# A two-workload kernel on one NeuronCore: the place of the Exp pass, of the attention copies and of one product in its rounds

## The chip, the cores and the metric

The kernel runs on one core of one Trainium2 chip. The metric is the device time in microseconds. Of the kernel before there are three timed runs (948.39, 950.51 and 950.9 us) and one profiled execution.

## The reference

Two independent computations share one launch. The first is chunked softmax attention, without a link between chunks:

```python
scores = scale * np.matmul(q_c, k_c.transpose(0, 1, 2, 4, 3))   # 8 x 8 x 9 chunks of 64 x 64
scores = scores - np.max(scores, axis=-1, keepdims=True)
attn = np.exp(scores)
attn = attn / (np.sum(attn, axis=-1, keepdims=True) + 1e-09)
out = np.matmul(attn, v_c)
```

Its result, turned to 4608 tokens of 512, is the input of the second:

```python
gate = 1.0 / (1.0 + np.exp(-(x @ w_gate)))      # 512 -> 1536
val = x @ w_val
return (gate * val @ w_out).astype(np.float32)  # 1536 -> 512
```

All values are float32. Every product of the second part is made of three matmuls over halves of the numbers (high x high, high x low, low x high).

## The kernel before

The tokens form nine blocks of 512. Blocks 0 to 2 are computed directly: for each of 12 slices `f` of the hidden width, `up` (L264) makes the gate and the value product, 12 matmuls each, `hidden` (L270) makes sigmoid times value and its two halves, and `down` (L290) adds 12 matmuls of the output product into four PSUM banks. `evacuate` (L297) copies them out (`ob`, L308).

Blocks 3 to 8 form three groups `n` of two blocks. A group replaces eight products of 2 x 2 parts by seven (numbered 1 to 7), on sums of operands and of weights that are made beforehand. The twelve rounds `i` of a group are its six values of `p`, each for `which` = 0 (gate) and 1 (value). A product is six matmuls of 128x512. A round runs on PE as `first` (products 1 and 6 into the banks `cx` and `cy`), then `last` of the round before (3 and 4), then `middle` (7, 2 and 5; product 5 has a PSUM bank of its own, `cz`, of which there is one). On ACT a round has the copy `s1` (L463) of product 1 and, where `which` is 0, four sigmoids (L495, L514). DVE adds: `u2` (L465), `u3` (L492), `c22` (L498), `c12` and `c21` (L508, L511). In odd rounds a gate product follows each (L475), three of the four on POOL. After the rounds `outward` (L526) does the output product, 252 matmuls at L579, from 21 operands that `prepare` casts (ACT, L551 and L559), takes the low half of (DVE, L552 and L560) and combines in place (DVE, L568).

Attention and the making of the next group's operands run beside all this. `flow` (L637) is a generator of small pieces in a fixed order. For two units of 512 x 512 it yields the score products `sc`, maximum and subtraction (L659, L660), the Exp pass (L663), sums and normalisation (L681 to L686), two transposes (L690), sixteen copies into `pbd` (L701 on POOL, L703 on ACT), the value products `av` (L234) and their copy (L245). Then come `differ` and `operands` (L407, L414) for the next group. `tick` (L714) spends credits, a number of each place in a round (`SHARES`), on these pieces; `insert` (L729) puts the products of attention between those of a round. Words such as "piece" or "wait" hold a piece back until a tick has passed, pairs such as ("up", n) until a group or a round is reached.

The order of PE, DVE and ACT is the order in which the program is written. The order of POOL and of SP, which issues all DMAs one after the other, is set by a scheduler. `keep_sums` (L334) is POOL's: it makes the sums of weights, some as `a_both` during blocks 1 and 2, the late ones as `a_late` in group 0, and SP stores them to DRAM. SP loads a round's weights (`wr`, L387 and L390) one round ahead. ACT loads another function table (ACT_TABLE_LOAD) between a sigmoid and an Exp.

Of the kernel before, what the change touches and what calls it, by code (L numbers as in the profile page):

```python
# [43 lines left out]

SHARES = {1: 2.7, 2: 3.0, "first": 0.7, "last": 2.0, "middle": 2.5, "down": 0.8}

# [4 lines left out]
def chunk_attn_moe(ctx: ExitStack, tc: tile.TileContext, q, k, v, w, out, outt):  # L51
# [362 lines left out]
    def operands(n):  # L414


        low = None
        for i, (name, (u, b), less) in enumerate(MADE):
            if i in (2, 5):
                yield from lower(*low)  # L420
                low = None
                yield ("open" if i == 2 else "up", n)
            at = raw[n, u][:, :, b]
            if less:
                (u0, b0), (u1, b1), op = less
                yield 1.2
                nc.vector.tensor_tensor(out=at, in0=raw[n, u0][:, :, b0], in1=raw[n, u1][:, :, b1], op=op)
            t = wp.tile([P, 2, 2, TB], F32R, tag=f"u{i}", name="xc")
            nc.scalar.copy(t[:, 0], at)
            if low:  # L430
                yield from lower(*low)
            low = n, name, t, at
        yield from lower(*low)
# [43 lines left out]
    def middle(n, p, which):  # L477
# [5 lines left out]
        if (p, which) == (0, 0):  # L483
            z = banks.pop((n, "z"), None) or sole(n, p, which)
            product(n, p, which, 2, x, False, True)
            product(n, p, which, 7, y, False, True)
        else:
            product(n, p, which, 7, y, False, True)
            product(n, p, which, 2, x, False, True)
            z = sole(n, p, which)  # L490
        u3 = mp.tile([P, TB], F32, tag="ob", name="u3")
        nc.vector.tensor_tensor(out=u3, in0=y, in1=s1, op=ALU.add)  # L492
        c22 = inner(n, f + 1, 1) if which == 0 else u3
        if which == 0:
            nc.scalar.activation(inner(n, f, 0), x, AF.Sigmoid)  # L495
        else:
            gated(n, f, 0, x, nc.vector)
        nc.vector.tensor_tensor(out=c22, in0=z, in1=u3, op=ALU.add)  # L498
        if which:
            gated(n, f + 1, 1, u3)  # L500
        banks[n, p, which] = y, z, s1, u2

# [23 lines left out]
    def outward(n, before_last):  # L526
# [14 lines left out]
        def prepare(i):  # L541
# [20 lines left out]
            if i == 3:  # L562
                reduce_hidden(n, 2, nc.vector)
            if i in (3, 4, 5, 9, 10, 11, 15, 16, 17):
                b11, t1x, b21, t2x = hid[n, i % 3]
                o, x, y, op = (
                    (b11, t2x, b11, ALU.subtract), (b21, b21, t2x, ALU.subtract), (t1x, t2x, t1x, ALU.add))[i // 6]
                nc.vector.tensor_tensor(out=o, in0=x, in1=y, op=op)  # L568
# [47 lines left out]
        for i in range(21):  # L616
# [6 lines left out]
            if i == 17 and n + 1 < 3:  # L623
                places[:] = [t2, t4, t0, t1, t3]
                load_group(n + 1, 0, 0)
            if i < 18:
                tick(SHARES["down"])
# [9 lines left out]
    def flow():  # L637
# [3 lines left out]
        for j in range(8, 4 * NB + 2, 2):  # L641
            more = j < 4 * NB
            joined = now["joined"]
            if more:
# [11 lines left out]
                for i in range(2):  # L656
# [4 lines left out]
                        out=pr[:, i], in0=scv[i], in1=mx.unsqueeze(2).broadcast_to([P, 8, D]), op=ALU.subtract)  # L661
                pr = pr.rearrange("p u g k -> p (u g) k")
                nc.scalar.activation(pr, pr, AF.Exp, scale=0.125)  # L663
            if kept and not (more and joined):
# [29 lines left out]
            for n in range(16):  # L694
                if n % 8 == 0:
                    yield "piece"
# [8 lines left out]
    ahead = flow()  # L705
    now = dict(credit=0.0, ticks=0, since=0, unit=8, early=-1, open=-1, up=-1, joined=False)
    now["item"] = next(ahead)
# [5 lines left out]

    def tick(share):  # L714
        now["ticks"] += 1
        now["credit"] += share
        while now["item"] is not None:
            if isinstance(now["item"], float):
                if now["credit"] < now["item"] / 2:
                    return  # L720
                now["credit"] -= now["item"]
            elif not (now["item"] == "piece" and now["ticks"] > now["since"]
                      or now["item"] == "wait" and now["ticks"] > now["since"] + (not now["joined"])
                      or now["item"][0] in ("early", "open", "up") and now["item"][1] <= now[now["item"][0]]):
                break
# [61 lines left out]
    def rest():  # L787
        for m in range(1, FIRST_PAIR):
            upto = 4 * (m + 2) if m == 1 else 4 * (m + 3)
            for f in range(2 if m == 1 else 0, NF):  # L790
                if m == 2 and f == 7:
                    now["early"] = now["open"] = now["up"] = 0
                step(m, f, "")
                tick(SHARES[m])
                insert(upto, 2)
                finish()
                tick(SHARES[m])
                insert(upto, 2)
                x = 12 * m + f - 13
                keep(min(32, (17 * x) // 10 if x < 11 else 17 + (17 * (x - 10)) // 10))  # L800
                if m == 2:
# [3 lines left out]
        for n in range(3):  # L805
            now["joined"], now["up"] = True, n
            upto = 4 * (FIRST_PAIR + 2 * n + 4)
            order = [(p, which) for p in range(6) for which in range(2)]
            due(n, 5)
            for i, (p, which) in enumerate(order):  # L810
# [11 lines left out]
                if i:  # L822
                    tick(SHARES["first"])
                    insert(upto, 1)
                    last(n, *order[i - 1])
                    if i == 10:
                        ending = outward(n, lambda: last(n, *order[-1]))
                        next(ending)
                    tick(SHARES["last"])
                    insert(upto, 1)  # L830
# [3 lines left out]
                if i == 11:  # L834
                    now["open"] = n + 1
                if n == 0 and i in (1, 2):
                    keep(32 + 2 * i, True)
                if 0 < i < 11:
                    tick(SHARES["middle"])
                    insert(upto, 1)  # L840
            next(ending, None)
# [37 lines left out]
```

## Time and profile before

| | us |
|---|---|
| timed runs, median (lowest to highest) | 950.51 (948.39 to 950.9) |
| profiled execution, its own time | 952.24 |
| its span in the trace | 950.5 |
| PE busy in the span | 913.1 (96%) |
| DVE, ACT, POOL busy | 577.5, 428.6, 320.4 |
| mean granted clock of PE, of full speed | 0.986 |

The profile shows one execution. In a timeline row stand the start, the duration of the merged instructions, the engine, the line, the operation with output and input, the number of instructions, and in brackets the idle time of the engine just before with what released it. PE's loads of weights (PEld) overlap its matmuls.

### The profile page before, as it was taken

What the parts mean: (1) busy time and instruction counts of PE and PEld (TensorE: products, weight loads), DVE (VectorE), ACT (ScalarE), POOL (GpSimd) and SP (SyncE); (2) the same over time, 40 slices, a digit from 0 to 9 for tenths busy, and PEclk for the clock granted to TensorE, in tenths of its full rate; (3) what the DMA queues carried; (4) which work ended last, traced back from release to release, by engine and by line L of the source; (5) the groups of instructions that cost most, each with busy time, mean ns of one, the idle gap of its engine ahead of it and who ended that gap; (6) DMA issues with size and microseconds to landing.
All of it is one profiled execution on the core that took longest, in us unless ns stands there. A gap on an engine that the chain in (4) does not pass through costs nothing.

```text
span 950.5 us, 13156 instructions
## 1 busy us (share of the span) xinstructions
PE 913.1 (96%) x4852; PEld 746.3 (79%) x4852; DVE 577.5 (61%) x818; ACT 428.6 (45%) x740; POOL 320.4 (34%) x421
## 2 busy tenths in 40 slices
PE   6999999999999997999999899999998999999998
PEld 4788788888888886887777788877777888888786
DVE  6889873454343458355557976455668854344784
ACT  6799652545545552344434432344435422113341
POOL 1000007999269979563330000242410001423000
PEclk7999999999999999999999899999999999999999
DMA  8698894445443465786654468764434685554563
GB/s 288 200 305 281 303 319 135 131 141 159 117 150 111 156 199 204 235 288 204 196 203 142 161 228 283 236 211 169 173 127 167 217 302 180 201 182 169 169 230 111
DMA packets 90544, 189.62 MB, mean 200 GB/s; under 512 B 7920, under 2 KB 49392, under 8 KB 86640
## 3 DMA queue, kind: packets, MB, share of 16 engines
q1 hardware_dynamic: 90480, 188.78, 59.9%
q8 instruction: 39, 0.64, 0.3%
q14 instruction: 25, 0.20, 0.1%
HBM read 146.28 MB, written 42.47 MB: 199 GB/s over the span
## 4 chain that ended last, share of the span: by engine, by line
PE 75%; DVE 9%; ACT 5%; DMA 5%; issue 2%; SPq 1%; POOL 1%; ACTq 0%; DVEq 0%
PE d L579 18%; PE g L264 14%; PE cy L447 13%; PE cz L447 9%; PE cx L447 9%; PE acc L290 6%; PE sc L173 3%; PE av L234 3%; DMA w_raw<-w_in 2%; DVE pr L660 1%; DMA given<-w 1%; DVE mx L659 1%; DVE w L139 1%; DMA wr<-sums 1%; ACT pr L663 1%
## 5 line engine op out<-in xcount | busy, mean ns | idle before, releaser
L264 PE MATMUL g<-xt,w 128*128 128x512 f32 (+1 forms) x960 | 209.2, 372 | 3.2 <-ACT hf L273 1.1
L264 PEld LDWEIGHTS g<-xt,w 128*128 128x128 f32 x960 | 168.3, 190 | 38.7 <-ACT hf L273 3.2
L579 PE MATMUL d<-hd,wd 128*128 128x512 f32 x756 | 177.4, 396 | 4.9 <-ACT hd L559 3.6
L579 PEld LDWEIGHTS d<-hd,wd 128*128 128x128 f32 x756 | 144.9, 192 | 37.0 <-ACT hd L559 4.4
L447 PE MATMUL cy<-xc,wr 128*128 128x512 f32 x648 | 161.9, 392 | 9.3 <-DVE s1u L465 5.2
L447 PEld LDWEIGHTS cy<-xc,wr 128*128 128x128 f32 x648 | 121.3, 188 | 37.0 <-DVE s1u L465 6.9
L475 POOL TENSOR_TENSOR hid<-u,hid 128x512 f32<-128x512 f32 x15 | 19.3, 1289 | 299.8 <-DVE u L498 299.6
L447 PE MATMUL cz<-xc,wr 128*128 128x512 f32 x432 | 111.3, 393 | 8.1 <-DVE u L498 6.0
L447 PE MATMUL cx<-xc,wr 128*128 128x512 f32 x432 | 111.3, 393 | 0.0
L290 PE MATMUL acc<-w,hx 128*128 128x512 f32 x432 | 106.2, 393 | 0.0
L352 POOL TENSOR_TENSOR a_val<-w 128x256 f32<-128x256 f32 x64 | 48.4, 777 | 165.0 <-DVE pbd L223 141.5
L447 PEld LDWEIGHTS cz<-xc,wr 128*128 128x128 f32 x432 | 80.1, 188 | 29.3 <-DVE u L498 8.5
L447 PEld LDWEIGHTS cx<-xc,wr 128*128 128x128 f32 x432 | 81.7, 190 | 17.8 <-issue 0.7
L290 PEld LDWEIGHTS acc<-w,hx 128*128 128x128 f32 x432 | 79.9, 188 | 18.0 <-issue 1.4
L275 DVE TENSOR_TENSOR hf<-g,hf 128x512 f32<-128x512 f32 (+1 forms) x40 | 25.4, 635 | 99.5 <-PE g L264 71.5
L559 ACT CAST hd<-hid 128x1024 fp32r<-128x1024 f32 x48 | 49.9, 1051 | 50.7 <-PE d L579 47.8
L560 DVE TENSOR_TENSOR hd<-hid,hd 128x1024 fp32r<-128x1024 f32 x48 | 58.4, 1224 | 18.6 <-ACT hd L559 18.6
L703 ACT COPY pbd<-pr 32x256 f32<-32x256 f32 x160 | 64.5, 403 | 11.4 <-DVE pr L690 9.5
L465 DVE TENSOR_TENSOR s1u<-cy,s1u 128x512 f32<-128x512 f32 x36 | 24.8, 688 | 72.1 <-PE cy L447 63.2
L463 ACT COPY s1u<-cx 128x512 f32<-128x512 f32 x36 | 21.0, 583 | 81.4 <-PE cx L447 81.4
L514 ACT ACTIVATE hid<-hid 128x512 f32<-128x512 f32 x54 | 33.3, 631 | 40.2 <-DVE hid L508 33.5
L475 POOL TENSOR_TENSOR hid<-s1u,hid 128x512 f32<-128x512 f32 x30 | 41.2, 1376 | 22.3 <-DVE s1u L508 21.6
(120 smaller groups left out, 1153.3 us busy)
## 6 DMA issues: line engine op xcount, KB each, us to landing
wr<-sums SPq DMA_DIRECT2D x72, 512.0 KB, 4.6
wd<-stream SPq DMA_DIRECT2D x30, 1024.0 KB, 4.8
w_raw<-w_in SPq DMA_DIRECT2D x36, 512.0 KB, 5.4
wr<-given SPq DMA_DIRECT2D x36, 512.0 KB, 3.7
sums<-a_both SPq DMA_DIRECT2D x24, 512.0 KB, 3.5
qt<-q_in SPq DMA_DIRECT2D x36, 256.0 KB, 4.1
kbd<-k_in SPq DMA_DIRECT2D x72, 128.0 KB, 3.9
vt<-v_in SPq DMA_DIRECT2D x36, 256.0 KB, 4.0
```

The lines of the kernel that those rows point to most:

```text
L173: nc.tensor.matmul(sc[c * D:(c + 1) * D, (2 * a + t) * P:(2 * a + t + 1) * P], lhsT=s["qt"][:, a, n0:n0 + D], rhs=s["kb"][:, a, :, n0:n0 + D],
L234: nc.tensor.matmul(av[a * D:(a + 1) * D, c * P:(c + 1) * P], lhsT=s["vt"][:, a, c, :], rhs=pb[:, 4 * a + c, :, :], start=True, stop=True,)
L264: nc.tensor.matmul(ps[:, tok], lhsT=wt[f, which][:, wpart, c:c + P], rhs=x[:, part, i, tok], start=n == 0, stop=n == 11)
L290: nc.tensor.matmul(acc[m, t], lhsT=hx[:, ts], rhs=wt[f, 2][:, wpart], start=f == 0 and i == 0, stop=f == NF - 1 and i == 2,)
L352: nc.gpsimd.tensor_tensor(out=dst, in0=parts[:, 0], in1=parts[:, 1], op=ALU.add)
L447: nc.tensor.matmul(bank, lhsT=lhs(wpart, c), rhs=x[:, part, c], start=start and k == 0, stop=stop and k == 5, skip_group_check=True)
L475: eng.tensor_tensor(out=h, in0=value, in1=h, op=ALU.mult)
L514: nc.scalar.activation(h, h, AF.Sigmoid)
L559: nc.scalar.copy(t[:, 0], at)
L560: nc.vector.tensor_tensor(out=t[:, 1], in0=at, in1=t[:, 0].bitcast(F32), op=ALU.subtract)
L579: nc.tensor.matmul(bank, lhsT=w[:, o:o + P], rhs=x[:, part], start=p == 0 and opening and i == 0, stop=p == 5 and i == 2, skip_group_check ...
L703: nc.scalar.copy(pb[dst, :, c, h, i, :], ps[src, h::2, k, :])
```

## The change

Five things are different.

A round of a group has three ticks, "first", "last" and "middle". In `flow`, a mark "apart" now stands ahead of the Exp pass, and `tick` doesn't pass it at "middle", only at the other two. The copies into `pbd` are one piece where groups run instead of two, and are kept from "middle" in the same way. In blocks 1 and 2 `insert` waits for one tick instead of two.

In `tick`, the credits of "last", "middle" and "down" are higher. The operands 6 and 7 of a group's seven wait for a mark "late" of their own.

In the last round of a group, product 5 comes ahead of product 2, and the gate on DVE behind both sums.

In `outward`, the first three in-place subtractions come at operands 5 to 7 instead of 3 to 5, and the ticks begin at `i` = 5.

Two of the weight sums that were made during block 2 are made as late ones in group 0: three late pairs instead of two.

```diff
@@ -42,7 +42,7 @@
-SHARES = {1: 2.7, 2: 3.0, "first": 0.7, "last": 2.0, "middle": 2.5, "down": 0.8}
+SHARES = {1: 2.7, 2: 3.0, "first": 0.7, "last": 2.4, "middle": 2.8, "down": 1.0}
@@ -419,7 +419,7 @@
                 low = None
-                yield ("open" if i == 2 else "up", n)
+                yield ("open" if i == 2 else "late", n)
             at = raw[n, u][:, :, b]
@@ -486,18 +486,23 @@
             product(n, p, which, 7, y, False, True)
-            product(n, p, which, 2, x, False, True)
+            if (p, which) != (5, 1):
+                product(n, p, which, 2, x, False, True)
             z = sole(n, p, which)
+            if (p, which) == (5, 1):
+                product(n, p, which, 2, x, False, True)
         u3 = mp.tile([P, TB], F32, tag="ob", name="u3")
...
             nc.scalar.activation(inner(n, f, 0), x, AF.Sigmoid)
-        else:
+        elif p < 5:
             gated(n, f, 0, x, nc.vector)
...
             gated(n, f + 1, 1, u3)
+            if p == 5:
+                gated(n, f, 0, x, nc.vector)
         banks[n, p, which] = y, z, s1, u2
@@ -561,10 +566,11 @@
                 reduce_hidden(n, 2, nc.vector)
-            if i in (3, 4, 5, 9, 10, 11, 15, 16, 17):
-                b11, t1x, b21, t2x = hid[n, i % 3]
+            if i in (5, 6, 7, 9, 10, 11, 15, 16, 17):
+                b11, t1x, b21, t2x = hid[n, (i - 5) % 3 if i < 9 else i % 3]
                 o, x, y, op = (
-                    (b11, t2x, b11, ALU.subtract), (b21, b21, t2x, ALU.subtract), (t1x, t2x, t1x, ALU.add))[i // 6]
+                    (b11, t2x, b11, ALU.subtract), (b21, b21, t2x, ALU.subtract), (t1x, t2x, t1x, ALU.add))[
+                        (i > 8) + (i > 14)]
                 nc.vector.tensor_tensor(out=o, in0=x, in1=y, op=op)
@@ -623,7 +629,7 @@
                 load_group(n + 1, 0, 0)
-            if i < 18:
+            if 4 < i < 18:
                 tick(SHARES["down"])
@@ -660,6 +666,7 @@
                 pr = pr.rearrange("p u g k -> p (u g) k")
+                yield "apart"
                 nc.scalar.activation(pr, pr, AF.Exp, scale=0.125)
@@ -692,7 +699,7 @@
             for n in range(16):
-                if n % 8 == 0:
+                if n == 0 or n == 8 and not now["joined"]:
                     yield "piece"
@@ -703,7 +710,7 @@
     ahead = flow()
-    now = dict(credit=0.0, ticks=0, since=0, unit=8, early=-1, open=-1, up=-1, joined=False)
+    now = dict(credit=0.0, ticks=0, since=0, unit=8, early=-1, open=-1, late=-1, up=-1, joined=False, place="")
     now["item"] = next(ahead)
@@ -711,7 +718,8 @@
-    def tick(share):
+    def tick(share, place=""):
+        now["place"] = place
         now["ticks"] += 1
@@ -719,9 +727,10 @@
                 now["credit"] -= now["item"]
-            elif not (now["item"] == "piece" and now["ticks"] > now["since"]
+            elif not (now["item"] == "piece" and now["ticks"] > now["since"] and now["place"] != "middle"
+                      or now["item"] == "apart" and now["place"] != "middle"
                       or now["item"] == "wait" and now["ticks"] > now["since"] + (not now["joined"])
-                      or now["item"][0] in ("early", "open", "up") and now["item"][1] <= now[now["item"][0]]):
+                      or now["item"][0] in ("early", "open", "late", "up") and now["item"][1] <= now[now["item"][0]]):
                 break
@@ -789,21 +798,21 @@
                 if m == 2 and f == 7:
-                    now["early"] = now["open"] = now["up"] = 0
+                    now["early"] = now["open"] = now["late"] = 0
                 step(m, f, "")
                 tick(SHARES[m])
-                insert(upto, 2)
+                insert(upto, 1)
                 finish()
                 tick(SHARES[m])
-                insert(upto, 2)
+                insert(upto, 1)
                 x = 12 * m + f - 13
-                keep(min(32, (17 * x) // 10 if x < 11 else 17 + (17 * (x - 10)) // 10))
+                keep(min(30, (17 * x) // 10 if x < 11 else 17 + (3 * (x - 10)) // 2))
                 if m == 2:
...
         for n in range(3):
-            now["joined"], now["up"] = True, n
+            now["joined"], now["late"], now["up"] = True, n, n
             upto = 4 * (FIRST_PAIR + 2 * n + 4)
@@ -820,24 +829,22 @@
                 if i:
-                    tick(SHARES["first"])
-                    insert(upto, 1)
+                    tick(SHARES["first"], "first")
                     last(n, *order[i - 1])
...
                         next(ending)
-                    tick(SHARES["last"])
+                    tick(SHARES["last"] if i < 11 else 1.2, "last")
                     insert(upto, 1)
...
                     now["open"] = n + 1
-                if n == 0 and i in (1, 2):
-                    keep(32 + 2 * i, True)
+                if n == 0 and i in (1, 2, 3):
+                    keep(30 + 2 * i, True)
                 if 0 < i < 11:
-                    tick(SHARES["middle"])
-                    insert(upto, 1)
+                    tick(SHARES["middle"], "middle")
             next(ending, None)
```

**Group 0, round 4, on ACT and DVE.** The names carry the number of the tile: `s1u_4195` before and `s1u_4190` now are the pair of `s1` and `u2` of round 5 (value part of `p` = 2); `pr` holds the attention scores. ACT before:

```order
L495 ACTIVATE hid<-cx 128x512
L663 ACT_TABLE_LOAD
L663 ACTIVATE pr<-pr 128x1024
L463 COPY s1u_4195<-cx 128x512
L514 ACT_TABLE_LOAD
L514 ACTIVATE hid<-hid 128x512 x3
L703 COPY pbd<-pr 32x8x32 x4
L463 COPY s1u_4275<-cx 128x512
L703 COPY pbd<-pr 32x8x32 x4
```

ACT now:

```order
L498 ACTIVATE hid<-cx 128x512
L463 COPY s1u_4190<-cx 128x512
L670 ACT_TABLE_LOAD
L670 ACTIVATE pr<-pr 128x1024
L519 ACT_TABLE_LOAD
L519 ACTIVATE hid<-hid 128x512 x3
L463 COPY s1u_4263<-cx 128x512
L710 COPY pbd<-pr 32x8x32 x8
L245 COPY raw<-av 128x2x256 x2
```

The copy `s1u` moved ahead of the table load and Exp, and the eight copies into `pbd` are together behind the next round's copy. DVE in the same stretch, before:

```order
L465 TENSOR_TENSOR s1u_4195<-cy,s1u_4195 128x512
L681 TENSOR_REDUCE sums_4204<-pr 128x16
L682 TENSOR_SCALAR sums_4204<-sums_4204 128x16
L684 RECIPROCAL inv_4207<-sums_4204 128x16
L686 TENSOR_TENSOR pr<-pr,inv_4207 128x1024
L508 TENSOR_TENSOR hid<-cz,s1u_4061 128x512
L511 TENSOR_TENSOR hid<-cy,s1u_4061 128x512
L690 STREAM_TRANSPOSE pr<-pr 128x512 x2
L492 TENSOR_TENSOR u_4248<-cy,s1u_4195 128x512
L475 TENSOR_TENSOR hid<-cx,hid 128x512
L498 TENSOR_TENSOR u_4248<-cz,u_4248 128x512
L465 TENSOR_TENSOR s1u_4275<-cy,s1u_4275 128x512
```

DVE now:

```order
L465 TENSOR_TENSOR s1u_4190<-cy,s1u_4190 128x512
L513 TENSOR_TENSOR hid<-cz,s1u_4049 128x512
L516 TENSOR_TENSOR hid<-cy,s1u_4049 128x512
L688 TENSOR_REDUCE sums_4217<-pr 128x16
L689 TENSOR_SCALAR sums_4217<-sums_4217 128x16
L691 RECIPROCAL inv_4220<-sums_4217 128x16
L693 TENSOR_TENSOR pr<-pr,inv_4220 128x1024
L495 TENSOR_TENSOR u_4242<-cy,s1u_4190 128x512
L475 TENSOR_TENSOR hid<-cx,hid 128x512
L501 TENSOR_TENSOR u_4242<-cz,u_4242 128x512
L697 STREAM_TRANSPOSE pr<-pr 128x512 x2
L465 TENSOR_TENSOR s1u_4263<-cy,s1u_4263 128x512
```

The softmax (L681 to L686 before) moved behind the two sums of `last`, and the transposes moved behind the three passes of `middle`.

**The late pairs on POOL and SP.** `a_late` is a late sum of weights, `hid<-u` and `hid<-s1u` are gates, `pbd` the attention copies. POOL before, the end of its second pair and what follows:

```order
L360 TENSOR_TENSOR a_late<-a_late 128x128 x2
L363 CAST a_late<-a_late 128x4x128
L364 TENSOR_TENSOR a_late<-a_late 128x4x128
L475 TENSOR_TENSOR hid<-s1u_3728,hid 128x512 x2
L701 COPY pbd<-pr 32x8x32 x8
L475 TENSOR_TENSOR hid<-u_4034,hid 128x512
L475 TENSOR_TENSOR hid<-s1u_3987,hid 128x512
```

POOL now, the end of its third pair:

```order
L360 TENSOR_TENSOR a_late<-a_late 128x128 x4
L363 CAST a_late<-a_late 128x4x128
L364 TENSOR_TENSOR a_late<-a_late 128x4x128
L475 TENSOR_TENSOR hid<-u_4003,hid 128x512
L708 COPY pbd<-pr 32x8x32 x8
L475 TENSOR_TENSOR hid<-s1u_3951,hid 128x512
L528 TENSOR_TENSOR hid<-hid 128x1024
```

Between the gates of round 1 (on `s1u_3692`) and the gate on `u_4003` of round 3 POOL now has two whole pairs, 32 instructions; before, one pair stood ahead of the gates of round 1 and none behind them. SP now, with the first pair's stores (`stream<-a_late`) and the weights of round 1 (`given_1779`):

```order
L387 DMA wr<-given_1698 128x512
L390 DMA wr<-sums_1702 128x1024
L387 DMA wr<-given_1779 128x1024
L390 DMA wr<-sums_1783 128x1024
L371 DMA stream<-a_late 128x2x256 x4
L387 DMA wr<-given_1779 128x512
L390 DMA wr<-sums_1783 128x1024
L309 DMA out<-ob 128x512 x2
```

Before, the four loads of round 1's weights stood together ahead of the stores; the second two are now behind them.

## Rows read from the trace of the kernel before

**Rows 1.** the page: busy us of each engine (share), its instructions

```profile
PE 913.1 (96%) x4852; PEld 746.3 (79%) x4852; DVE 577.5 (61%) x818; ACT 428.6 (45%) x740; POOL 320.4 (34%) x421
```

**Rows 2.** PE's waits; columns: who waits for whom, us in total, times, longest us

```profile
PE cz L447 <- DVE u L498: 6.0, 6, 1.2
...
PE cy L447 <- DVE s1u L465: 5.2, 3, 1.7
PE cy L447 <- DVE ob L308: 4.0, 1, 4.0
PE d L579 <- ACT hd L559: 3.6, 2, 1.8
...
PE d L579 <- DVE hd L560: 1.3, 2, 0.8
...
PE cz L447 <- ACT hf L273: 1.0, 1, 1.0
...
PE cz L447 <- DVE hid L508: 0.9, 2, 0.4
```

**Rows 3.** stretches: length, busy us of PE, PEld, DVE, ACT, POOL, clock, DMA

```profile
434.00:436.00 2.00, 0.61 (x3) 0.18 (x1) 0.40 (x1) 1.97 (x4) 0.00 (x0) 1.00 0.39 80
...
528.00:536.00 8.00, 7.41 (x19) 5.49 (x20) 8.00 (x9) 4.83 (x7) 0.00 (x0) 0.57 0.27 112
...
378.00:382.00 4.00, 4.00 (x12) 3.12 (x12) 0.69 (x1) 0.36 (x1) 1.01 (x1) 0.58 0.54 184
```

**Rows 4.** stretches, L579 alone: length, PE, PEld, clock, DMA share, GB/s

```profile
515.09:578.02 62.93, 60.54 (x252) 48.96 (x251) 0.95 0.59 200
712.00:773.80 61.80, 59.24 (x252) 48.20 (x251) 0.97 0.61 206
889.53:946.82 57.29, 57.28 (x252) 47.12 (x251) 1.00 0.52 179
```

**Rows 5.** timeline, group 0: start, us, engine, line, operation, xcount, idle before

```profile
432.74 1.28 ACT L663 ACT_TABLE_LOAD   x1 [4.30 <-DVE pr L660]
...
434.04 1.06 ACT L663 ACTIVATE pr<-pr 128x1024 f32<-128x1024 f32 x1
...
435.00 0.57 ACT L463 COPY s1u<-cx 128x512 f32<-128x512 f32 x1
...
435.60 0.69 DVE L465 TENSOR_TENSOR s1u<-cy,s1u 128x512 f32<-128x512 f32 x1 [2.96 <-ACT s1u L463]
436.20 1.21 DVE L681 TENSOR_REDUCE sums<-pr 128x16 f32<-128x1024 f32 x1
...
436.34 1.67 PE L447 MATMUL cy<-xc,wr 128*128 128x512 f32 x6 [1.74 <-DVE s1u L465]
...
437.94 1.22 DVE L686 TENSOR_TENSOR pr<-pr,inv 128x1024 f32<-128x1024 f32 x1
...
440.29 1.29 DVE L690 STREAM_TRANSPOSE pr<-pr 128x512 f32<-128x512 f32 x2
...
441.74 3.46 POOL L701 COPY pbd<-pr 32x256 f32<-32x256 f32 x8 [13.68 <-DVE pr L690]
...
445.28 1.29 POOL L475 TENSOR_TENSOR hid<-u,hid 128x512 f32<-128x512 f32 x1
```

**Rows 6.** timeline, handover from block 2 to group 0

```profile
364.11 2.40 POOL L352 TENSOR_TENSOR a_late<-w 128x256 f32<-128x256 f32 x2
...
376.28 0.65 DVE L308 COPY ob<-acc 128x512 f32<-128x512 f32 x1
...
376.98 2.19 PE L447 MATMUL cy<-xc,wr 128*128 128x512 f32 x6 [4.02 <-DVE ob L308]
```

**Rows 7.** timeline of POOL, a late pair in group 0

```profile
394.68 1.43 POOL L352 TENSOR_TENSOR a_late<-w 128x256 f32<-128x256 f32 x2
...
404.62 2.55 POOL L475 TENSOR_TENSOR hid<-s1u,hid 128x512 f32<-128x512 f32 x2
```

**Rows 8.** instructions by line: busy us, mean ns, idle before

```profile
L437 DVE TENSOR_TENSOR xc<-raw,xc 128x1024 fp32r<-128x1024 f32 x21 | 26.9, 1310 | 0.0
```

## The prediction

> **What bounds the kernel now.** I read the page's busy line first: TensorE (PE) is busy for 96% of the span [rows 1], so a gain can only be idle time of PE or time at its low clock. The second view is PE's own waits, longest first [rows 2]. Each line is to be read as "who kept PE waiting, how often, how long". The third is the granted clock of short stretches [rows 3], since a wait may be paid for twice, as idle time and as slow products behind it. The fourth sets the three output stages beside each other [rows 4], which are the same 252 matmuls in three surroundings. The undisturbed one gives the unit of this text: 57.28 us / 252 = 0.227 us per matmul, 1.364 us for a product of six. The timelines come last [rows 5 to 7], to see what stood ahead of the late instruction on its own engine.
>
> What the edits can reach lies in four of PE's waits. (1) In group 0 a copy `s1u` stands behind the Exp pass on ACT: table load, Exp at 434.04 for 1.06, copy only at 435.00, DVE's sum at 435.60, PE resumes at 436.34 after 1.74 us [rows 5]. (2) The single bank of product 5 is freed by DVE's `u` sum, which comes late six times. (3) At the handover from block 2 to group 0, DVE copies a finished bank out (`ob`, 376.28) only after a softmax, and PE waits 4.02 us [rows 6]. (4) In the output stage the casts of the hidden operands stand behind casts for the next group [rows 2, 4].
>
> **What goes, by its rows.** The sum is made against the profiled execution, 952.24 us (span 950.5).
> Handover: 4.0 (`ob`) and 1.0 (`hf`) of waits. The stretch 378 to 382 ran at a granted clock of 0.58, partly at 1.2 GHz, after PE had stood for 4.02 us: 4 x 0.42 = 1.7. In the new order the operands are made earlier, the two `ob` copies stand ahead of the softmax, and nothing that waits is between. Sum 6.7.
> Groups 0 and 1: 5.2 (`s1u`), 0.9 (`hid`) and 6.0 (`u`) of waits, eleven times. The product after such a wait has 1.67 us in its row, where six matmuls at the full rate are 1.364; of these 0.3 us I take 0.2 as refilling, 0.2 x 11 = 2.2. The copy `s1u` now stands ahead of the table load and Exp, and the softmax comes behind the two sums of `last`, so these go. The three of the six `u` waits that fall in last rounds go because product 5 now runs before product 2, and its bank is read one product earlier. Sum 14.3. The 1.74 us waits left the clock at 1.00 [rows 3], so nothing is given back there.
> Output stages 0 and 1: 62.93 and 61.80 us against 57.29 without the next group's operands [rows 4]. 5.6 + 4.5 = 10.1, of which 4.9 are waits [rows 2] and the rest is clock: 8 us at 0.57 are 3.4 us in the first alone [rows 3].
> All of it: 6.7 + 14.3 + 10.1 = 31.1 us. It is an upper bound, as nothing else of PE's idle time is touched.
>
> **What comes in its place.** I walked the new order with the old durations, with a product at 1.364 us and each engine in order.
> (a) Operand casts in block 2. Five of them now stand ahead of a sigmoid `hf`; the fifth needs six DVE passes of about 1.31 us [rows 8], 7.9 in all. With a cast of about 1.06 (the Exp pass has its width) and a sigmoid of about 0.57 that is 9.5, where PE asks for a new `hf` every 36 matmuls, 8.2 us. 1.3 us late, and I take 1.5 with the refill; between 0 (passes at the 1.22 of DVE's calm rows) and 3.
> (b) SP. A weight load of round 1 now stands behind four stores of the late pair, which wait for POOL. It lands about when it is needed: 0.6, between 0 and 3. The same holds for round 4's sums behind the next pair, which by the walk land 0.5 us early: nothing, up to 3.
> (c) POOL in group 0. Three late pairs instead of two come after the groups begin. One pair took from 394.68 to 404.62, 9.9 us [rows 7]. Two now lie in one piece ahead of the gate on `u` and of the eight `pbd` copies. Counted from round 2's first product, the pairs run from 7.7 (behind two gates) to 17.7 and from 18.8 (the buffer must be stored first) to 28.9, the gate ends at 30.1, the copies at 33.6. PE wants these for `av` at 28.2, after 18 products (24.6) and one attention insert of 64 matmuls a quarter as wide (3.6). So 5.4 us of waiting in place of cover that was ample before. As after the 4.02 us wait, I add the clock, 1.7, and 0.3 of refill: 7.4. Between 2 (the pairs run while DVE is quiet and the store is quick) and 11.
> (d) The other attention steps of the groups. The transposes now stand behind `u`, a gate and the last sum of the odd round. From that round's first product: the Exp pass ends at about 5.95, the softmax chain (436.20 to 439.16, 2.96) follows the sums of `last` at 6.3 and ends at 9.2, three passes of up to 0.69 end at 11.1, POOL's gate of 1.29 at 12.5, eight copies of 3.46 at 16.0 [rows 5]. PE reaches `av` after eleven products, at 15.0. So 1.0 late, 1.1 with the refill, five times: 5.5. If DVE had no queue, the gate could start at 10.4 and `av` would be 0.2 late; that is the lower end, 1. At the upper end each wait lowers the clock as after the longer waits, and it is 5 x (1.1 + 1.7) = 14. I stay at 5.5, since 1.74 us of idle did not lower it [rows 3]. Two further `av` of round 2 are just in time: 0.3.
> (e) The output stages. The in-place subtractions are two operands later, which keeps the early casts clear, and DVE is full up to the twelfth operand: its low half is about 0.7 late. 0.7 x 2 = 1.4, between 0 and 6 if the clock falls again.
> Sum 1.5 + 0.6 + 7.4 + 5.8 + 1.4 = 16.7. Block 1's shifted attention costs nothing by the walk (its copies are 1.7 us ahead of use); the cover is ACT's idle time there.
>
> 952.24 - 31.1 + 16.7 = 937.8. The profiled run is 1.7 above the median of the runs shown, 950.51, so about 936 for a median.
>
> **A rule that speaks against the edit.** In the trace a switch of ACT's table is one load of 1.28 us, and Exp starts 0.02 after its end [rows 5]. The Trainium skill (ScalarE: Activation LUTs, section "What ACT_TABLE_LOAD costs") adds a drain of about 1.38 us to each load. The trace doesn't show one at this place. By the page, Exp would end 1.4 later, and the five `av` waits with it: about 7 more, 943.
>
> **The rivals.**
> *Most of the new waits stay hidden.* The walk gives DVE and POOL every queue at its worst; if (d) stays at 1 and (c) at 2, with 3 for the rest, it is 952.24 - 31.1 + 6 - 1.7 = 925. For it: POOL is busy for a third of the span [rows 1]. Against: the pair of 9.9 us and the eight copies are in one queue.
> *The clock falls at each `av`.* (d) becomes 14 and (e) 6, so 936 + 8.5 + 4.6 = 949, which is no change. For it: 4.02 us of waiting cost 1.7 in clock, and 1.8 with a shorter wait behind it cost 3.4. Against: 1.74 alone cost none.
> *POOL's copies become the bound: slower.* POOL's `a_late` sum took 1.20 us beside DVE's passes over two operands in the handover [rows 6] and 0.72 later on [rows 7], 1.7 times as long. If the eight copies stretch like that, 3.46 becomes 5.8, each of six `av` waits grows by 2.3 and, being over 3 us, brings 1.7 of clock: 6 x 4 = 24, hence 960. It decides from 17 us on, which is 2.9 per `av`. Against it: the 3.46 was measured with three DVE passes beside it. The Trainium skill (GPSIMD Engine Reference, section "1. Specifications") says that POOL shares its access to SBUF with DVE, in conflict when DVE reads two operands from SBUF. The `a_late` rows agree; the DVE passes beside the copies read one from PSUM.
> *It doesn't do what it says*: a wait is only renamed, `s1u` or `ob` still come late, and the time is as before. The new order of ACT and DVE excludes it for `s1u`; little is left.
>
> **Chances and range.** Forecast 0.52 (928 to 943); hidden 0.19; clock at each `av` 0.15; copies 0.09; the drain 0.02; renamed 0.03. What a measurement here can tell is about 0.3%, 2.9 us: faster is below 947.7, slower above 953.4. Faster: 0.52 + 0.19 + 0.02, a third of the clock case, 0.05, and a little of the copies, 0.02: 0.80. Same: 0.08 of the clock case, the renamed case and 0.01 of the copies: 0.12. Slower: the rest, 0.08. The range 923 to 949 holds the forecast, most of the hidden case and half of the clock's, about 0.78.
>
> **What would show it.** In the new profile: PE's lines `cy <- DVE s1u`, `cy <- DVE ob` and `d <- ACT hd` gone, `cz <- DVE u` down to nothing, the output stages of groups 0 and 1 near 58. The new lines would be `av <- POOL pbd`, one of about 5 us in group 0 and five of about 1, and `cz` or `g <- ACT hf` of 1 to 2. If `av` has no line, the first rival holds; if stretches behind the `av` rows show a clock near 0.57, the second; if the copies take over 5 us, the third. If `d <- ACT hd` stands as before, my reading of the output stage is wrong.

## The result and the profile after

The changed kernel takes 936.85 us (median of 4 runs, 934.49 to 941.56) against 950.66 (4 runs, 948.39 to 950.9). The ratio is 0.9866, with a 95% interval of 0.9824 to 0.9909: 13.8 us, 1.3% faster. The forecast was 936 with a range of 923 to 949. The profiled execution is the slowest of the four, 941.56 us with a span of 939.8, so a comparison of the two profiles shows 10.7 us.

PE's waits of the profile after, to be set beside [rows 2] (who waits for whom, us in total, times, longest us):

```profile
PE av L234 <- POOL pbd L708: 8.1, 7, 4.2
...
PE sc L173 <- DMA kbd<-k_in: 4.1, 4, 1.7
PE av L234 <- DVE pr L666: 3.6, 4, 1.4
PE g L264 <- ACT hf L273: 3.2, 2, 2.3
```

No line of [rows 2] is left: `cy <- s1u`, `cy <- ob`, `cz <- u` and `d <- hd` are gone. `av` for POOL's `pbd` is the line that was forecast; `av` for DVE's `pr` was not, nor were 1.95 of the 4.1 us of `sc` for `kbd`. The other 2.1 stand in the first 8 us of the kernel, where the profile before has 1.5. The output stages, L585 alone (length, PE, PEld, clock, DMA share, GB/s), answer to [rows 4]:

```profile
518.52:575.99 57.47, 57.43 (x252) 47.03 (x251) 1.00 0.65 223
706.80:764.25 57.45, 57.41 (x252) 47.03 (x251) 1.00 0.65 223
878.85:936.12 57.27, 57.26 (x252) 47.11 (x251) 1.00 0.52 179
```

57.5 us instead of 62.93 and 61.80. The timelines give the time of each stage, from the first product of one to the first of the next:

| stage | before | after | difference | forecast |
|---|---|---|---|---|
| blocks 0 to 2, to the first `cz` | 366.9 | 376.3 | +9.5 | +0.5 |
| rounds of group 0 | 148.2 | 142.2 | -6.0 | -3.5 |
| output stages 0 and 1 | 124.7 | 114.9 | -9.8 | -8.7 |
| rounds of group 1 | 134.0 | 130.8 | -3.2 | -1.8 |
| rounds of group 2 | 115.7 | 114.6 | -1.1 | -1.0 |

The last column divides the prediction's terms over the stages. They sum to -14.5 and the measured differences to -10.6. So the total came out by two errors of opposite sign, which is in part luck: in this profile the direct blocks lost 9 us that were not forecast, the groups and the output stages gained some 5 more than forecast. The 376.3 us are the highest of their kind: four of the versions below have the same program up to the first `cz`, and their profiles show 368.9, 372.1, 373.0 and 373.0, a loss of 2 to 6 us. In blocks 1 and 2 the rows are these (PE in the timeline; DVE's passes over the scores):

```profile
184.80 1.97 PE L173 MATMUL sc<-kbd,qt 128*64 128x128 f32 x32
...
195.25 0.69 DVE L666 TENSOR_TENSOR pr<-sc,mx 128x512 f32<-128x512 f32 x1
...
196.08 1.09 PE L234 MATMUL av<-pbd,vt 128*64 128x128 f32 x16 [0.93 <-DVE pr L666]
196.57 0.69 DVE L666 TENSOR_TENSOR pr<-sc,mx 128x512 f32<-128x512 f32 x1
...
197.40 1.09 PE L234 MATMUL av<-pbd,vt 128*64 128x128 f32 x16 [0.23 <-DVE pr L666]
```

In the profile before, the same two products are:

```profile
185.26 1.97 PE L173 MATMUL sc<-kbd,qt 128*64 128x128 f32 x32
...
200.98 1.97 PE L234 MATMUL av<-pbd,vt 128*64 128x128 f32 x32
```

`av` comes 11.3 us after the scores `sc`; before, it came 15.7 us after them. The two PSUM banks that it needs still hold the scores until L666 has read them at 195.25 and 196.57, and PE waits 0.93 and 0.23. The `kbd` loads of the next scores (SP's queue, then PE):

```profile
212.75 18.53 SPq L367 DMA_DIRECT2D sums<-a_both  x4
...
237.13 1.09 PE L173 MATMUL sc<-kbd,qt 128*64 128x128 f32 x16 [1.50 <-DMA kbd<-k_in]
```

SP issues these loads only at 232.0, behind four stores of weight sums that wait for POOL. PE now asks for them at 235.6 and waits 1.50 and, for the second, 0.45 us. ACT later in block 2:

```profile
356.64 1.04 ACT L429 CAST xc<-raw 128x1024 fp32r<-128x1024 f32 x1 [3.58 <-DVE raw L427]
357.59 0.59 ACT L273 ACTIVATE hf<-g 128x512 f32<-128x512 f32 x1
```

Here the fifth cast waits 3.58 us for DVE, and the sigmoid `hf` starts at 357.59. PE waits 2.32 us for it, and the clock falls behind that (stretch, busy us of five engines, clock, DMA share, GB/s):

```profile
356.00:360.00 4.00, 1.76 (x7) 1.43 (x8) 2.84 (x4) 2.16 (x3) 0.00 (x0) 0.95 0.97 257
360.00:364.00 4.00, 4.00 (x13) 3.15 (x12) 4.00 (x5) 1.32 (x2) 0.00 (x0) 0.62 0.96 363
424.00:428.00 4.00, 0.00 (x0) 0.00 (x0) 0.63 (x1) 0.38 (x1) 3.81 (x6) 0.98 0.59 153
428.00:432.00 4.00, 2.83 (x24) 2.44 (x26) 0.00 (x0) 0.54 (x1) 3.66 (x7) 0.50 0.91 280
432.00:436.00 4.00, 4.00 (x46) 3.79 (x43) 0.00 (x0) 0.64 (x2) 4.00 (x3) 0.66 1.03 405
```

The last three rows are round 4 of group 0, where `av` waits for POOL. POOL's timeline:

```profile
403.10 1.43 POOL L352 TENSOR_TENSOR a_late<-w 128x256 f32<-128x256 f32 x2
...
413.59 1.43 POOL L352 TENSOR_TENSOR a_late<-w 128x256 f32<-128x256 f32 x2 [0.47 <-DMA stream<-a_late]
...
425.03 1.26 POOL L475 TENSOR_TENSOR hid<-u,hid 128x512 f32<-128x512 f32 x1
426.35 3.46 POOL L708 COPY pbd<-pr 32x256 f32<-32x256 f32 x8
```

PE in the same stretch:

```profile
428.10 0.69 PE L234 MATMUL av<-pbd,vt 128*64 128x128 f32 x4 [4.20 <-POOL pbd L708]
429.86 3.25 PE L234 MATMUL av<-pbd,vt 128*64 128x128 f32 x28 [1.07 <-POOL pbd L708]
```

The first pair runs from 403.10 to about 413.1, the second from 413.59, the gate follows at 425.03, the eight copies end at 429.8, and PE has waited 4.20 and 1.07 us. In the rounds behind it the wait is short, as the timeline of all engines shows:

```profile
450.18 0.68 DVE L501 TENSOR_TENSOR u<-cz,u 128x512 f32<-128x512 f32 x1
...
450.78 1.29 DVE L697 STREAM_TRANSPOSE pr<-pr 128x512 f32<-128x512 f32 x2
...
451.01 1.29 POOL L475 TENSOR_TENSOR hid<-u,hid 128x512 f32<-128x512 f32 x1 [13.86 <-DVE u L501]
...
452.37 3.46 POOL L708 COPY pbd<-pr 32x256 f32<-32x256 f32 x8
...
454.91 0.44 PE L234 MATMUL av<-pbd,vt 128*64 128x128 f32 x4
...
455.88 1.75 PE L234 MATMUL av<-pbd,vt 128*64 128x128 f32 x28 [0.53 <-POOL pbd L708]
```

Last sum, transposes, POOL's gate and its eight copies follow one another as walked, and end at 455.83. PE has four matmuls of `av` to do on the first copies, and waits 0.53 us for the last.

### The profile page after: what moved, and what is told of

Same layout as the page of the kernel before. It is cut to its first block, busy times and chain, and to the rows that moved or that the text cites. A ratio compares the mean times of both kernels' runs of the same rounds, so it can differ in the third digit from the quotient of the medians.

```text
span 939.8 us, 13164 instructions
## 1 busy us (share of the span) xinstructions
PE 907.8 (97%) x4852; PEld 745.6 (79%) x4852; DVE 572.0 (61%) x818; ACT 428.5 (46%) x740; POOL 317.1 (34%) x421
## 4 chain that ended last, share of the span: by engine, by line
PE 71%; POOL 11%; DVE 7%; DMA 5%; ACT 3%; issue 2%; SPq 1%; POOLq 0%; DVEq 0%; ACTq 0%
PE d L585 18%; PE g L264 13%; PE cy L447 12%; PE cz L447 8%; PE cx L447 8%; PE acc L290 5%; PE av L234 3%; PE sc L173 3%; DMA sums<-a_both 2%; POOL pbd L708 2%; POOL a_both L364 2%; POOL a_sum L360 2%; POOL a_val L352 2%; POOL hid L475 1%; DMA w_raw<-w_in 1%
## 5 line engine op out<-in xcount | busy, mean ns | idle before, releaser
L585 PE MATMUL d<-hd,wd 128*128 128x512 f32 x756 | 172.4, 389 | 0.1
L585 PEld LDWEIGHTS d<-hd,wd 128*128 128x128 f32 x756 | 141.7, 188 | 30.3 <-DVE hd L565 0.9
L708 POOL COPY pbd<-pr 32x256 f32<-32x256 f32 x64 | 25.2, 394 | 107.6 <-DVE pr L697 104.8
L495 DVE TENSOR_TENSOR u<-cy,s1u 128x512 f32<-128x512 f32 x36 | 24.7, 685 | 56.0 <-PE cy L447 56.0
L234 PE MATMUL av<-pbd,vt 128*64 128x128 f32 x576 | 40.3, 290 | 11.8 <-POOL pbd L708 8.1
```

The source lines that it names most:

```text
L234: nc.tensor.matmul(av[a * D:(a + 1) * D, c * P:(c + 1) * P], lhsT=s["vt"][:, a, c, :], rhs=pb[:, 4 * a + c, :, :], start=True, stop=True,)
L585: nc.tensor.matmul(bank, lhsT=w[:, o:o + P], rhs=x[:, part], start=p == 0 and opening and i == 0, stop=p == 5 and i == 2, skip_group_check ...
L708: nc.gpsimd.tensor_copy(pb[dst, :, c, h, i, :], ps[src, h::2, k, :])
```

## The experiments

Each is run beside the kernel before on one chip; its median was 950.68, 949.48 and 951.12 us in the three sessions, each on another chip. The changed kernel itself was timed in a session of its own (950.66).

**Two ticks in blocks 1 and 2.**

```diff
-                insert(upto, 1)
+                insert(upto, 2)
                 finish()
...
-                insert(upto, 1)
+                insert(upto, 2)
```

> The changed kernel with one part undone: in blocks 1 and 2 the attention products wait for two ticks again instead of one. Theory: in the changed kernel's trace, the waits of av for the reader of the score bank (L666, 4 times, 3.6 us), of sc for kbd (about 2 us) and the longer wait for hf (2.3 us, with the clock at 0.85 to 0.98 behind it, about 1.7 us) all come from products that are put one tick earlier. Then these go, a wait for hf of about 1 us as before the change remains, and the time falls by 6 to 8 us, from 936.9 to about 930. Rival: the waits come from the changed order of SP's and POOL's work (two sums fewer in block 2); then they stay and the time stays at 937.

933.22 us (930.25 to 936.25), ratio 0.9822 (0.979 to 0.9854). PE's waits:

```profile
PE cz L447 <- DVE hid L501: 2.9, 1, 2.9
...
PE g L264 <- ACT hf L273: 0.2, 1, 0.2
```

The line of `av` for the scores' reader is gone; it is at 3.6 to 4.0 us in every profile here with one tick and in none with two. `hf` is at 0.2, and `kbd` at 1.7, all of it in the first 8 us of the kernel. The stage of blocks 0 to 2 takes 364.5 us instead of 376.3. So the one tick was the cause of the waits for the scores' reader, and the rival falls; `kbd` and `hf` vary between runs of one program. But a wait of 2.9 us is new (`cz`, below), and the median falls by 3.6 us, not by 6 to 8; the intervals of the two ratios overlap, so the time alone doesn't show the gain.

**Two late pairs.**

```diff
-                keep(min(30, (17 * x) // 10 if x < 11 else 17 + (3 * (x - 10)) // 2))
+                keep(min(32, (17 * x) // 10 if x < 11 else 17 + (17 * (x - 10)) // 10))
...
-                if n == 0 and i in (1, 2, 3):
-                    keep(30 + 2 * i, True)
+                if n == 0 and i in (1, 2):
+                    keep(32 + 2 * i, True)
```

> The changed kernel with two late pairs of weight sums in group 0 instead of three (two more sums made in block 2). Theory: the wait of av for pbd of 4.2 + 1.1 us in round 4 of group 0, with the low clock behind it, comes from two whole pairs in POOL's queue; with one pair it goes, and the time falls by 6 to 7 us to about 930. Rival: it comes from the later transposes, as in the other rounds; then a wait of over 3 us stays and the time is within 2 us of 936.9. A possible cost: POOL is busier in block 2 and round 1's weights come up to 3 us late.

934.8 us (931.55 to 937.15), ratio 0.9834 (0.9807 to 0.9861). PE's waits:

```profile
PE av L234 <- DVE pr L666: 3.7, 4, 1.2
PE av L234 <- POOL pbd L708: 3.2, 6, 0.5
...
PE cz L447 <- DVE hid L501: 1.8, 1, 1.8
```

The long wait of `av` is gone; six of at most 0.5 us are left. The rounds of group 0 take 136.8 us instead of 142.2, with a new wait of `cz` (1.8 us, below) among them. The median falls by 2.0 us only, not by 6 to 7, and the intervals overlap: the profile shows that the pair was the cause of the long wait, the time alone doesn't.

**Both.** The two edits together.

> Both of these edits at once in the changed kernel: products wait for two ticks in blocks 1 and 2, two late pairs. If the two causes are separate, their gains add: 924 to 925. If one POOL or SP queue is behind both, the gain is that of one of them, about 930.

926.4 us (924.37 to 930.14), ratio 0.9752 (0.9726 to 0.9779): 10.4 us below the changed kernel, with intervals that don't overlap. The medians of the single versions fell by 3.6 and 2.0 us, 5.7 together. In the profiles the first output stage begins at 518.5 us in the changed kernel, at 509.7 and 510.8 in the single versions and at 503.2 here: 8.8, 7.7 and 15.3 us earlier. So it is not one gain counted twice. Whether the two add exactly is open: blocks 0 to 2 alone differ by several us between runs of one program. The new wait of `cz` is seen here with its chain:

```profile
370.63 5.53 SPq L371 DMA_DIRECT2D stream<-a_late  x4
...
376.26 0.94 SPq L309 DMA_DIRECT2D out<-ob  x2
...
379.05 0.69 DVE L495 TENSOR_TENSOR u<-cy,s1u 128x512 f32<-128x512 f32 x1 [6.48 <-DMA out<-ob]
...
380.52 1.67 PE L447 MATMUL cz<-xc,wr 128*128 128x512 f32 x6 [3.31 <-DVE hid L501]
```

DVE's `u` sum (L495) of round 0 waits 6.48 us for the DMA `out<-ob`: its output takes the ring buffer from which `ob` is stored. SP issues that store at 376.26, behind four stores of the first late pair, which it holds for 5.53 us while POOL makes them. PE waits 3.31 us at the end of this chain. In the two single versions the same sum waits for the same store, 6.05 and 4.95 us.

**A buffer of its own for `ob`**, on top of both:

```diff
-        if 0 < m < FIRST_PAIR - 1 or t < 2:
+        if m == FIRST_PAIR - 1 and t < 2:
+            ob = mp.tile([P, DM], F32, tag="hf" if t == 0 else "ob", name="ob", **({"bufs": 1} if t == 0 else {}))
+        elif 0 < m < FIRST_PAIR - 1 or t < 2:
```

> The version with two ticks in blocks 1 and 2 and two late pairs, and one more edit: of the last direct block's two rows of output tiles that are copied out through the ring of two ob buffers, one goes through the buffer of hf, so that u3 of round 0 finds a free ob buffer. Theory: in that version the wait of cz for DVE's sum (3.3 us) is a chain: u3 waits for the store of ob, which stands in SP's queue behind four stores of a late pair, which wait for POOL. Then the wait goes and the time falls from 926.4 by 3 to 4 us to about 923. Rival: u3 is late for DVE's queue or for the product itself; then the wait stays at about 3 us, and the time at 926.

924.66 us (924.19 to 926.84), ratio 0.9748 (0.9719 to 0.9777). The wait of `cz` for DVE's sum is gone from PE's list, and the rounds of group 0 take 136.1 us instead of 139.1. That shows the chain. The time doesn't show the gain: the median is 1.7 us lower, in another session, and the ratio is the same as in the version before it (0.9752). Blocks 0 to 2 differ from run to run by as much (367.9 here, 364.1 there).

**Without the mark at the Exp pass**, on the changed kernel:

```diff
                 pr = pr.rearrange("p u g k -> p (u g) k")
-                yield "apart"
                 nc.scalar.activation(pr, pr, AF.Exp, scale=0.125)
```

> The changed kernel without the mark that holds the Exp pass away from the tick behind the middle products. Theory: the copy s1u stands behind the Exp pass again, cy waits for DVE's s1u three or more times (5 to 6 us with refilling, and the waits for u in group 1 of about 4 us may return), while the short waits of av for pbd (0.5 each) go: 940 to 944. Rival: it was the later softmax and the copies in one piece that took these waits away; then the time stays within 2 us of 936.9.

945.51 us (942.34 to 949.55), ratio 0.9946 (0.9921 to 0.9972). Of PE's waits:

```profile
PE cy L447 <- DVE s1u L465: 12.2, 7, 1.7
...
PE cz L447 <- DVE hid L513: 3.1, 6, 0.9
```

The time lies above the 940 to 944 that were expected. The waits for `s1u` are back, and seven instead of three: group 1 now has them too, in place of its waits for `u`. Its rounds take 136.8 us instead of 130.8. So this mark is worth 8.7 us between the medians of two sessions, and the joined copies, which stay, don't do it without it. The later softmax was not tried by itself: without the mark it falls back as well, ahead of the two sums of `last` (L687 at 436.14, L513 at 439.02), and the `hid` waits return with it. For `s1u` the timeline names the Exp pass: DVE waits 2.96 us for the copy, which follows Exp directly on ACT (Exp at 433.97, copy at 434.93), as in [rows 5].

**Early subtractions, early ticks, both.** Three kernels on the output stage of the changed one. First the subtractions alone:

```diff
-            if i in (5, 6, 7, 9, 10, 11, 15, 16, 17):
-                b11, t1x, b21, t2x = hid[n, (i - 5) % 3 if i < 9 else i % 3]
+            if i in (3, 4, 5, 9, 10, 11, 15, 16, 17):
+                b11, t1x, b21, t2x = hid[n, i % 3]
```

> The changed kernel with the first three in-place subtractions of the output stage back at operands 3 to 5; all else stays. The prediction's reading: the later subtractions keep the early casts clear, so the waits of d for ACT's and DVE's hd come back in output stages 0 and 1, each goes from 57.5 to 62 or 63, and the time rises by 8 to 10 us to about 946. Rival: the stall came from the next group's operand casts that stood ahead of the hd casts on ACT, which wait for DVE; then these stages stay within 1 us of 57.5 and the time at 937.

937.6 us (936.78 to 938.77), ratio 0.9881 (0.9853 to 0.9909): no change. Then the ticks alone:

```diff
-            if 4 < i < 18:
+            if i < 18:
```

> The changed kernel with the ticks of the output stage beginning at its first step again instead of its sixth, so that the next group's operands are made between the early hd casts. The prediction's reading (subtractions): the output stages stay at 57.5 to 58.5 and the time within 2 us of 936.9. Rival (operand casts ahead of hd casts on ACT): stages 0 and 1 go back to 61 to 63 with waits of d for hd, and the time rises by 7 to 10 us to about 945.

941.16 us (940.24 to 943.58), ratio 0.9922 (0.9891 to 0.9952). Then both:

> The changed kernel with both edits of the output stage undone: in-place subtractions at operands 3 to 5 and ticks from the first step. Alone, the early subtractions left stages 0 and 1 at 57.3 us and the early ticks at 59.1. Theory: the stall needs both, since DVE's three extra passes of 1.22 us and the next group's operands together use up the lead of the hd casts; then stages 0 and 1 go back to 61 to 63 with waits of d for hd of 2 us or more, and the time to 945 to 949. Rival: only the ticks count and the rest of the old stall came from the credits; then the stages stay at 59 to 59.5 and the time at 941.

945.64 us (944.39 to 946.95), ratio 0.995 (0.9923 to 0.9977). The first output stage of the three, in the same order, each with L585 alone:

```profile
514.47:571.77 57.30, 57.30 (x252) 47.04 (x251) 1.00 0.65 222
```

```profile
513.78:572.89 59.11, 57.69 (x252) 47.03 (x251) 1.00 0.63 213
```

```profile
515.15:577.01 61.86, 59.30 (x252) 48.21 (x251) 0.97 0.61 205
```

57.3, 59.1 and 61.9 us. With both, the old stall is back, and ACT shows it as before the change:

```profile
518.76 1.99 ACT L429 CAST xc<-raw 128x1024 fp32r<-128x1024 f32 x2
525.95 1.05 ACT L429 CAST xc<-raw 128x1024 fp32r<-128x1024 f32 x1 [5.20 <-DVE raw L427]
526.90 1.99 ACT L564 CAST hd<-hid 128x1024 fp32r<-128x1024 f32 x2
```

The cast for the next group (L429) waits 5.20 us for DVE, and the `hd` casts stand behind it. With the early ticks alone it waits 4.06 us, and PE waits 0.66 and 0.76 us in each stage. The early subtractions put one more pass of 1.22 us on DVE ahead of it. So the early ticks make the wait and the early subtractions lengthen it: the later subtractions take most of the stall away, the later ticks all of it.

**Product 5 ahead of product 2 alone**, on the kernel before:

```diff
             product(n, p, which, 7, y, False, True)
-            product(n, p, which, 2, x, False, True)
+            if (p, which) != (5, 1):
+                product(n, p, which, 2, x, False, True)
             z = sole(n, p, which)
+            if (p, which) == (5, 1):
+                product(n, p, which, 2, x, False, True)
```

The gate on DVE goes behind both sums, as in the change.

> The kernel before with one part of the change alone: in the last round of a group product 5 ahead of product 2, and the gate on DVE behind both sums. Theory: the bank of product 5 is read one product (1.36 us) earlier, so the three waits of cz for DVE's u in the last rounds (0.8 each) go, the three of group 1 (1.2 each) stay; PE's line for them falls from 6.0 us in 6 to 3.7 in 3, and the time by 2 to 3 us to 948. Rival: DVE's queue, not the bank, is late there; then the line stays at six and the time at 950.7.

947.32 us (944.33 to 950.9), ratio 0.9975 (0.9956 to 0.9994), 2.2 us less than the kernel before. Of PE's waits:

```profile
PE cz L447 <- DVE u L501: 3.6, 3, 1.2
```

Three waits are left, those of group 1, as expected.

**Seven copies on POOL, nine on ACT**, on the version with `ob` apart:

```diff
-                if n % 2 and now["joined"]:
+                if n % 2 and n < 14 and now["joined"]:
```

> The version with two ticks in blocks 1 and 2, two late pairs and ob in a buffer of its own, and in a group seven copies into pbd on POOL and nine on ACT instead of eight and eight. Theory: av's second half waits for POOL's last copy (six waits of 0.5, 3.2 us); one copy less on POOL is 0.43 earlier, so these fall to 0.1 to 0.2 each and the time by 1.5 to 2.5 us, from 924.7 to about 922.7. Rival: ACT becomes the last, as its copies start behind the s1u copy; then av waits for ACT's pbd by as much or more, and the time is 924.7 or up to 2 us above.

925.71 us (923.07 to 927.51), ratio 0.9738 (0.9714 to 0.9761): the same. The rival holds, by PE's waits:

```profile
PE av L234 <- ACT pbd L712: 3.8, 6, 0.6
```

Now ACT has the last copy, and `av` waits for it six times, 3.8 us in all, where it waited 3.2 for POOL. So moving one more copy to ACT gains nothing.

## Why the prediction was right, and where it was not

**What goes.** All lines that the sum took away are gone. For two of them a run shows the cause that was given: `s1u` with `hid` (back without the mark at Exp) and `u` in the last rounds (gone with product 5 alone: 2.2 us, with 2.4 of waits and 0.6 of refilling taken). For `ob` the order speaks: DVE copies it at 378.63, and the softmax comes at 389.45; which edit moved it was not tried. The output stages gave 5.5 and 4.3 us for 5.6 and 4.5.

**The output stage's reason was wrong.** The prediction put the gain to the in-place subtractions being two operands later. With these undone nothing changes; the later ticks alone are enough. The (e) term, 1.4 us for a late twelfth operand, didn't come either.

**Block 1's attention was put at nothing.** "Block 1's shifted attention costs nothing by the walk" is the step that failed. I looked at the copies into `pbd` only, and not at the two PSUM banks, which `av` takes over from the scores: 3.6 us in four waits, two in block 1 and two in block 2. The `kbd` loads come late for the earlier products too, behind stores in SP's queue: 1.95 us in two waits here, and between 0 and 2.35 in the four versions with the same program up to there.

**(a) was right in its cause, and its size varies.** For `hf` I took 1.5 us and found one new wait of 2.32, with 1.7 of clock in the rows of 356 to 364 (the other wait of that line, 0.92, stands in block 0 and was 0.83 before). In the same four versions this wait is 1.25 to 1.50 us, and the clock stays at 1.00.

**(b) Nothing.** SP's queue cost nothing in the changed kernel's groups. The queue was a cost all the same, at a place that the prediction didn't name: the store of `ob` behind the late pair, 1.8 to 3.3 us in the three versions with two ticks, two late pairs or both. And in block 1 the `kbd` loads stand behind stores of weight sums.

**(c) was right in place and close in size.** 5.3 us of waiting for 5.4. The clock took 0.50 and 0.34 of the two stretches of 4 us behind it, up to 3.4, where 1.7 was taken. Two late pairs bring 5.4 to 6.1 us of the rounds of group 0 back.

**(d) was half.** The last copy came 1.0 us after `av` was due, as walked. But `av` has four matmuls that need only the first copies, and PE waits 0.53 to 0.68 us, five times 2.8 in all, for the 5.5 taken.

**The rivals.** At the five short waits the clock stayed at full speed, 1.00 in the 8 us around each (one is shown), and POOL's eight copies took 3.46 us as before:

```profile
455.00:463.00 8.00, 7.47 (x80) 6.45 (x81) 1.38 (x2) 2.19 (x5) 3.29 (x4) 1.00 0.72 224
```

ACT's table switch is one load each way, next to the passes that it serves:

```profile
443.57 1.28 ACT L670 ACT_TABLE_LOAD   x1 [1.51 <-DVE pr L666]
444.86 1.06 ACT L670 ACTIVATE pr<-pr 128x1024 f32<-128x1024 f32 x1
445.94 1.28 ACT L519 ACT_TABLE_LOAD   x1
```

The drain of the Trainium skill (ScalarE: Activation LUTs, section "What ACT_TABLE_LOAD costs") is not to be seen: Exp starts 0.01 us after the load's end, and the next load 0.02 after Exp's.

A version with two parts undone beats both kernels: 926.4 us, and 924.66 with a buffer of its own for `ob`. The higher credits, the copies in one piece and the mark "late" were not undone one by one; what each of these brings stays open.

## What to carry to other kernels

Where an engine in order feeds the bottleneck, look for the long independent instruction ahead of the short one that is waited for, and move that; here a mark at one Exp pass, which moves the softmax behind it too, was worth 8.7 us. Before moving a consumer earlier, list every buffer it takes over (here PSUM banks still being read), not only its inputs. And a change of several parts should be run with each part undone: here two of them together cost 10 us of what the others brought. Where a stage varies between runs, as blocks 0 to 2 do here, one profile is not enough to size a part.

## What the runs showed of the hardware

The length of a wait alone doesn't say whether the clock falls behind it. After 3.31 us of `cz`, up to 380.52 in the version with both parts undone, the clock stayed at full speed:

```profile
380.00:384.00 4.00, 3.48 (x15) 2.87 (x16) 3.86 (x7) 0.63 (x1) 0.00 (x0) 1.00 0.70 240
384.00:388.00 4.00, 4.00 (x20) 3.30 (x19) 3.96 (x7) 1.23 (x2) 1.18 (x4) 1.00 0.79 262
```

In the changed kernel it fell to 0.62 in the stretch from 360 to 364 behind the 2.32 us of `hf`, and to 0.50, which is 1.2 GHz, in the stretch with the waits of 4.20 and 1.07. The same wait for `hf` at 2.92 us (two late pairs) brought 0.59 in the stretch from 356 to 360, and at 1.25 to 1.50 us, in four other versions, it left the clock at 1.00. What tells the cases apart was not tried.
